# Side-by-side keys for one score product, paired global scores, and earlier q and k loads in a fused attention and expert kernel

## The chip, the cores and the metric

The kernel runs on one core of one Trainium2 chip. The metric is device time in microseconds (us) of one execution; before the change its median over three runs is 869.57 us (868.72 to 870.97). The core has five engines that run in parallel, each through its own list of instructions in order: TensorE (PE, matrix products; PEld is its loading of weights), VectorE (DVE), ScalarE (ACT), GpSimd (POOL), and SyncE (SP), which here only issues DMAs.

## The reference, cut to what matters

```
def _attn_ref(q, k, v, sampled_blocks):          # B, H, S, D = 4, 8, 768, 64; blocks of 32 rows
    scores = scale * np.matmul(q, k.transpose(0, 1, 3, 2))
    mask = np.abs(blk_i - blk_j) <= 1
    mask = mask | (blk_i == 0) | (blk_j == 0) | (blk_i == n_blocks - 1) | (blk_j == n_blocks - 1)
    mask[...] = True                              # and three sampled key blocks for each query block
    attn = softmax(np.where(mask, scores, -1e9))
    return np.matmul(attn, v)

def reference(...):
    x = attn_out.transpose(0, 2, 1, 3).reshape(B * S, H * D)
    return _moe_ref(x, ...)   # top-2 of 8 experts by x @ w_gate and noise, each relu(x @ w1[e]) @ w2[e]
```

A query block sees eight key blocks: its neighbours and itself (three), three sampled ones, and the first and the last. Queries of the first and last block (the global ones) see all 768 keys.

## The kernel before

The attention comes first and takes the first third of the time, then the experts. The work of attention is a list of items in fixed order (`items`, L64): for each batch 12 query items `("q", b, t, f)`, which are a tile `t` of 128 queries (four blocks) and a half `f` of the eight heads, and four global items `("g", b, i, par)`. There are 64 items, 16 to a batch. `steps` walks through them as a software pipeline with one step for each item. A step at item k first turns the probabilities of item k (`turn`, on PE, copied out by DVE and ACT), then computes the scores of item k+2 and their softmax (`scores`, `soft`), then the product with V of item k-1 (`av`) and its scaling (`norm`). Between these parts a router for the experts is woven in by small slices (`background`), and its table of one-hot products (`hot`, L748 on POOL, L757 on PE) shares POOL, DVE and PE with the attention.

The scores of a query item (`scores`, L232) are 16 products of 192 columns on 64 rows and 32 columns of the array (head dimension 64, one block of 32 queries), over two strips of the keys: the three neighbouring blocks and a copy of the three sampled blocks; and then four products of 64 columns on 64 rows and all 128 columns of the array for the first and last key block. Each float32 product stands as two instructions in the trace. A global item (`scores`, first branch) is four products of 384 columns on one half of the array's rows. Each item takes two of six PSUM banks for its scores.

POOL copies the sampled blocks of a tile two tiles ahead into rows behind the keys (`prefetch_k`, L194, three copies for each block) and scales q (L175). `soft` takes the maximum on DVE (L278, L269) and the exponential on ACT (L281, L273). SP issues all loads in program order: q (`prefetch_q`, L186), the keys of the next batch in six parts (`load_k`, L164), V of a tile in two halves (`prefetch_v`, L206 and L210), where a V tile may be loaded once the product that used its buffer three tiles earlier is done, and the stores of x (L589). For each block of queries V takes three loads of one block each, at a place that SP reads out of a register; 264 of SP's loads are of that kind. In the last batch there are two V buffers, and SP also issues the zero fill of the output (L1277) and the first expert weights (L852).

## Time and profile before

| what | us |
|---|---|
| median of three runs | 869.57 |
| the profiled execution's own time | 876.67 |
| its span, first to last instruction | 874.8 |
| PE busy | 812.1 |
| DVE busy | 562.1 |
| ACT busy | 357.9 |
| POOL busy | 346.6 |
| last score product of the attention (L232) starts | 301.3 |

An engine's list runs in order, so a wait on one instruction holds up all behind it. "x" counts instructions, a stretch gives start and length in us from the start of the span, and square brackets give the idle time before a row and what ended it. PEclk is the granted clock of TensorE as a share of 2.4 GHz.

### The profile page before, as it was taken

To read this page: it belongs to the slowest core of one execution; us is meant where nothing else is said; L and a number is where in the kernel's file an instruction comes from. 1 tells how busy PE (TensorE), PEld (TensorE's weight loads), DVE (VectorE), ACT (ScalarE), POOL (GpSimd) and SP (SyncE) were. 2 spreads that over 40 slices of the span, in tenths; PEclk is the share of its full clock that TensorE was granted. 3 is DMA by queue.
4 is the path that set the end of the run, shared out by engine and by line. 5 is a ranking of instruction groups with operands and counts; after the bars stand their busy time and mean duration, and the time that the engine had idled before them with its cause. 6 is when DMAs were issued, how large, how long until landed. Compare 5 with 4: busy or idle time off the path is not lost.

```text
span 874.8 us, 26176 instructions
## 1 busy us (share of the span) xinstructions
PE 812.1 (93%) x10207; PEld 513.8 (59%) x10207; DVE 562.1 (64%) x1197; ACT 357.9 (41%) x666; POOL 346.6 (40%) x584
## 2 busy tenths in 40 slices
PE   7988988989887869999989899999999999999996
PEld 5776776677665657565467454554554554554552
DVE  6576885888786537762123368688688697696631
ACT  4655654755654405321022242452452552642510
POOL 3444455545547330131133606516516426322311
PEclk7899998999999969999999999999999999999998
DMA  4677687667688895755139959729739629523301
GB/s 155 196 210 203 175 222 198 200 184 219 185 263 265 232 196 151 195 185 107 50 100 196 242 123 231 202 80 238 202 98 230 196 90 246 171 67 126 101 28 51
DMA packets 119847, 148.94 MB, mean 170 GB/s; under 512 B 69515, under 2 KB 76300, under 8 KB 119714
## 3 DMA queue, kind: packets, MB, share of 16 engines
q1 hardware_dynamic: 107490, 109.22, 48.1%
q0 software_dynamic: 12224, 37.96, 13.4%
q8 instruction: 82, 1.34, 0.6%
q14 instruction: 51, 0.42, 0.2%
HBM read 107.28 MB, written 26.15 MB: 153 GB/s over the span
## 4 chain that ended last, share of the span: by engine, by line
PE 71%; DVE 8%; issue 7%; SPq 6%; DMA 3%; POOL 2%; ACT 1%; another core or an unknown queue 1%; POOLq 1%; DVEq 0%; ACTq 0%
PE pc L1086 28%; PE pa L1039 9%; PE pa L1000 6%; PE ps L232 6%; PE pd L1039 5%; PE pd L1000 4%; SPq L210 4%; PE po L327 3%; PE pc L1039 2%; PE pc L1095 2%; DMA kk<-in_kt_dram 2%; DVE m L278 2%; PE ps L305 2%; PE po L397 1%
## 5 line engine op out<-in xcount | busy, mean ns | idle before, releaser
L1086 PE MATMUL pc<-w,hh 128*128 128x512 f16 x768 | 228.4, 379 | 0.0
L1119 POOL DMA_INDIRECT out_dram<-y,r_xT x46 | 66.9, 1454 | 216.4 <-DVE y L1118 179.1
L1086 PE MATMUL pc<-w,hl 128*128 128x512 f16 x384 | 145.5, 379 | 0.0
L1086 PEld LDWEIGHTS <-hh 128*128 128x128 f16 x768 | 74.5, 98 | 86.4
L1039 PEld LDWEIGHTS <-w 128*128 128x128 f16 x840 | 82.2, 98 | 63.1
L281 ACT ACTIVATE p<-ps,m 128x256 f32<-128x256 f32 x192 | 75.2, 474 | 80.2 <-DVE m L278 73.8
L278 DVE TENSOR_REDUCE m<-ps 128x2 f32<-128x512 f32 x96 | 61.7, 684 | 33.6 <-PE ps L232 33.5
L232 PE MATMUL ps<-kk,q 64*32 64x192 f32 (+1 forms) x1920 | 77.9, 340 | 4.6 <-POOL q L175 2.8
L194 POOL COPY kk<-kk 128x128 f32 x264 | 67.0, 303 | 37.8 <-DMA kk<-in_kt_dram 21.4
L1008 ACT ACTIVATE hh<-pa 128x408 f16<-128x408 f32 (+2 forms) x60 | 26.1, 447 | 123.8 <-PE pa L1000 104.1
L890 DVE SCALAR_TENSOR_TENSOR w<-wraw,w 128x1024 f16<-128x1024 f32 (+1 forms) x58 | 65.2, 1127 | 15.7 <-ACT w L886 15.7
L232 PEld LDWEIGHTS ps<-kk,q 64*32 64x32 f32 (+1 forms) x1920 | 52.5, 129 | 31.4 <-issue 20.4
L1011 DVE SCALAR_TENSOR_TENSOR hl<-pa,hh 128x408 f16<-128x408 f32 (+2 forms) x60 | 29.9, 503 | 60.1 <-ACT hh L1008 47.7
L327 PE MATMUL po<-va,ptr 128*32 128x68 f32 x1536 | 56.1, 235 | 9.6 <-DVE xr L337 2.8
L1086 PEld LDWEIGHTS <-hl 128*128 128x128 f16 x384 | 37.5, 98 | 45.3
L942 POOL DMA_INDIRECT xg<-x_rows,r_xT x46 | 57.2, 1242 | 14.7 <-issue 14.7
L960 POOL DMA_INDIRECT pv<-out_dram,r_xT x44 | 48.1, 1093 | 32.4 <-issue 29.8
L886 ACT ACTIVATE w<-wraw 128x1024 f16<-128x1024 f32 (+1 forms) x58 | 56.4, 975 | 7.0 <-DMA wraw<-in_moe_w_dram 7.0
L327 PE MATMUL po<-vb,ptr 128*32 128x68 f32 x1536 | 55.4, 232 | 1.9 <-issue 1.8
L1118 DVE SCALAR_TENSOR_TENSOR y<-pc,r_xT,pv 128x512 f32<-128x512 f32 x37 | 27.7, 750 | 45.0 <-PE pc L1086 45.0
L305 PE MATMUL ps<-r_ident,p 128*128 128x128 f32 x384 | 53.9, 283 | 2.3 <-ACT p L281 1.2
L1000 PEld LDWEIGHTS <-w1s 128*128 128x128 f16 x432 | 42.9, 100 | 19.1 <-issue 6.3
(229 smaller groups left out, 1531.2 us busy)
## 6 DMA issues: line engine op xcount, KB each, us to landing
wraw<-in_moe_w_dram SPq DMA_DIRECT2D x64, 512.0 KB
va<-in_vw_dram SPq DMA_DIRECT2D x40, 384.0 KB
vb<-in_vx_dram SPq DMA_DIRECT2D x176, 64.0 KB
q<-in_qt_dram SPq DMA_DIRECT2D x24, 256.0 KB
va<-in_vx_dram SPq DMA_DIRECT2D x88, 64.0 KB
kk<-in_kt_dram SPq DMA_DIRECT2D x18, 256.0 KB
x_rows<-x SPq DMA_DIRECT2D x16, 256.0 KB
out_dram<-zeros SPq DMA_DIRECT2D x4, 768.0 KB
```

What stands on the lines that cost most here:

```text
L194: nc.gpsimd.tensor_copy(kk[:, self.row(t, j) + n], flat[:, bass.ds(self.listed(t * self.NJ + j, n), P)])
L232: mm = lambda o, l, r: nc.tensor.matmul(o, l, r, start=True, stop=True, skip_group_check=True)
L278: nc.vector.tensor_reduce(m[:, par], s[par].rearrange("p (e c) -> p e c", e=2), axis=AX.X, op=ALU.max, negate=True)
L281: nc.scalar.activation(p[:, 2 * e + par], s[par][:, 256 * e:256 * e + 256], AF.Exp, bias=m[:, par, e:e + 1])
L305: nc.tensor.transpose(t[:, e, c], p[:, 2 * e + par, P * c:P * c + P], self.ident)
L327: nc.tensor.matmul(o[32 * j:32 * j + 32, h], d[:, h % 2, h // 2, x, 32 * j:32 * j + 32], self.values(v[:, self.slot(t, j)], 4 * f + h), st ...
L890: self.nc.vector.scalar_tensor_tensor(lo, t, WS, hi, op0=ALU.mult, op1=ALU.subtract)
L942: nc.gpsimd.indirect_dma_start(out=self.xg[0:m, c + self.place(u)], out_offset=None, in_=self.x_dram[0:nr], in_offset=bass.IndirectOffsetO ...
L1000: nc.tensor.matmul(ph[:, 0:m], w[:, wt, slot, kb % 2 * P:kb % 2 * P + P], r["xt"][:, kb, a, o:o + m], start=i == 0, stop=i == last)
L1039: nc.tensor.matmul(o, w[:, wt, slot, s * P:s * P + P], mv(s, a), start=i == 0 and p in tail, stop=i == 5, skip_group_check=True)
L1086: nc.tensor.matmul(py, h[:, f, o], w(f)[:, x], start=i == 0, stop=i == last)
L1119: d = nc.gpsimd.indirect_dma_start(out=self.out, out_offset=bass.IndirectOffsetOnAxis(ap=r["ix"][0:m, c:c + 1], axis=0), in_=y[0:m], in_of ...
```

## The change

Five things change. The keys that a block of queries sees lie side by side in new tiles `kc` (two, for even and odd tiles of queries): POOL copies three sampled blocks as before and one more piece of three neighbouring blocks, and ACT copies the first and last block, once for each batch and each of the two tiles. A query item's scores are then 16 products of 256 columns, and the four products of 64 columns are gone. The two global items of one `i` are scored in one step, with the products of both halves of the array's rows in turn, and the order of items is changed so that the four global items of a batch follow each other (in the first batch, one query item stands between the pairs). q is loaded a step earlier in most tiles and each part of the next batch's keys one step earlier. The rest makes room: `kk` is smaller, some tiles move between pools, and the zeros for the fill are made in an x buffer at step 49 in place of a tile of their own at step 18.

```diff
-            self.items += g[0:2] + q[0:1] + g[2:3] + q[1:2] + g[3:] + q[2:] if b == 0 else q[0:1] + g[0:3] + q[1:2] + g[3:] + q[2:]
+            self.items += g[0:2] + q[0:1] + g[2:] + q[1:] if b == 0 else q[0:1] + g + q[1:]
...
-        self.kk = [two(2 - 2 * i).tile([P, self.NB + 2 * J * 3, P], F32, name=f"kk{i}") for i in range(2)]
+        self.kk = [two(2 - 2 * i).tile([P, self.NB, P], F32, name=f"kk{i}") for i in range(2)]
+        self.kc = [self.buf.tile([P, J, self.NP, 8, 32], F32, name=f"kc{i}") for i in range(2)]
...
     def prefetch_k(self, b, t):
-        nc, kk = self.nc, self.kk[b % 2]
-        js = self.real(t)
+        nc, kk, kc, NB = self.nc, self.kk[b % 2], self.kc[t % 2], self.NB
         flat = kk.rearrange("p n c -> p (n c)")
-        for j in js:
+        turned = lambda x: x.rearrange("p e (n c) -> p n e c", c=32)
+        for j in self.real(t):
+            blk = t * self.NJ + j
             for n in range(3):
-                nc.gpsimd.tensor_copy(kk[:, self.row(t, j) + n], flat[:, bass.ds(self.listed(t * self.NJ + j, n), P)])
-
-    def row(self, t, j):
-        return self.NB + ((t % 2) * self.NJ + j) * 3
+                nc.gpsimd.tensor_copy(kc[:, j, :, 3 + n], flat[:, bass.ds(self.listed(blk, n), P)].rearrange("p (n c) -> p n c", c=32))
+            nc.gpsimd.tensor_copy(kc[:, j, :, 0:3], turned(kk[:, blk - 1:blk + 2]))
+        for j in range(self.NJ if t < 2 else 0):
+            nc.scalar.activation(kc[:, j, :, 6:8], turned(kk[:, 0:NB:NB - 1]), AF.Copy)
...
-            i, h = it[2], head(it[3])
-            qg = self.st["qg", b]
-            s = self.st[it, "s"] = [self.bank() for _ in range(2)]
+            i, qg = it[2], self.st["qg", b]
+            s = [[self.bank() for _ in range(2)] for _ in range(2)]
             for kh in range(2):
                 for e in range(2):
-                    mm(s[kh][64 * e:64 * e + 64, 0:384], qg[h, 2 * i + e, :],
-                       kk[h, NB // 2 * kh:NB // 2 * kh + NB // 2, 2 * i + e])
+                    for par in range(2):
+                        mm(s[par][kh][64 * e:64 * e + 64, 0:384], qg[head(par), 2 * i + e, :],
+                           kk[head(par), NB // 2 * kh:NB // 2 * kh + NB // 2, 2 * i + e])
+            for par in range(2):
+                self.st[it[:3] + (par,), "s"] = s[par]
             return
         _, b, t, f = it
         q = self.st["q", b, t]
         self.st[it, "s"] = [self.bank() for _ in range(2)]
         s = [x.rearrange("p (e c) -> p e c", e=2) for x in self.st[it, "s"]]
+        kc = self.kc[t % 2].rearrange("p j n e c -> p j n (e c)")
         for e in range(2):
             p = 2 * f + e
             for j in range(self.NJ):
-                blk = min(max(t * self.NJ + j - 1, 0), NB - 3)
                 for par in range(2):
-                    w = kk[head(par), blk:blk + 3, p]
-                    step = (self.row(t, self.slot(t, j)) - blk) * P
-                    w = bass.AP(tensor=w.tensor, offset=w.offset, ap=[list(w.ap[0]), [step, 2]] + [list(a) for a in w.ap[1:]])
-                    mm(s[par][32 * j:32 * j + 32, e, 0:192], q[head(par), p, 32 * j:32 * j + 32], w)
-        for e in range(2):
-            p = 2 * f + e
-            for par in range(2):
-                mm(s[par][:, e, 192:256], q[head(par), p, :], kk[head(par), 0:NB:NB - 1, p])
+                    mm(s[par][32 * j:32 * j + 32, e], q[head(par), p, 32 * j:32 * j + 32], kc[head(par), self.slot(t, j), p])
...
-            if new[0] != "none":
+            if new[0] == "q" or new[0] == "g" and new[3] == 1:
                 self.scores(new)
-                self.soft(new)
+                for par in range(2 if new[0] == "g" else 1):
+                    self.soft(new[:3] + (par,) if new[0] == "g" else new)
...
-            if new[0] == "q" and new[3] == 1:
-                for _ in range(1 + (nq == self.late_)):
-                    if nq < len(tg):
-                        self.prefetch_q(*tg[nq])
-                        nq += 1
+            if new[0] == "q" and nq < len(tg) and (nq > self.late_) == (new[3] == 1):
+                self.prefetch_q(*tg[nq])
+                nq += 1
...
-            if new[0] == "q" and new[1] + 1 < B and 0 < 2 * new[2] + new[3] - 1 <= 6:
-                self.load_k(new[1] + 1, 2 * new[2] + new[3] - 2, 6)
+            if new[0] == "q" and new[1] + 1 < B and 0 < 2 * new[2] + new[3] <= 6:
+                self.load_k(new[1] + 1, 2 * new[2] + new[3] - 1, 6)
...
+    at(PER * 3 + 1, lambda: nc.gpsimd.memset(spare(), 0.0))
```

In the first batch PE's list has this order from the first global scores on. The names are score banks (`ps`), keys (`kk`, `kc`), global queries (`qg`), queries (`q`), probabilities (`pg`, `p`); x8 and x4 count products. Before:

```order
L232 MATMUL ps<-kk_105,qg_107 64x384 x8
L293 MATMUL ps<-r_ident,pg 96x128 x8
L232 MATMUL ps<-kk_105,q 32x192 x16
L232 MATMUL ps<-kk_105,q 128x64 x4
L293 MATMUL ps<-r_ident,pg 96x128 x8
L232 MATMUL ps<-kk_105,qg_107 64x384 x4
L305 MATMUL ps<-r_ident,p 128x128 x8
L232 MATMUL ps<-kk_105,q 32x192 x16
L232 MATMUL ps<-kk_105,q 128x64 x4
L293 MATMUL ps<-r_ident,pg 96x128 x8
L232 MATMUL ps<-kk_105,qg_107 64x384 x4
L327 MATMUL po<-va_99,ptr 32x68 x4
```

and in the changed kernel, where L238 stands for L232, L294 for L293, L306 for L305 and L328 for L327:

```order
L238 MATMUL ps<-kk_105,qg_109 64x384 x8
L294 MATMUL ps<-r_ident,pg 96x128 x8
L238 MATMUL ps<-kc_107,q 32x256 x16
L294 MATMUL ps<-r_ident,pg 96x128 x8
L306 MATMUL ps<-r_ident,p 128x128 x8
L238 MATMUL ps<-kk_105,qg_109 64x384 x8
L294 MATMUL ps<-r_ident,pg 96x128 x8
L238 MATMUL ps<-kc_107,q 32x256 x16
L328 MATMUL po<-va_99,ptr 32x68 x4
```

The second pair of global scores is one group of eight, and behind it the turning of its first item follows with nothing between.

On SP's list, behind the last V load of the third tile, the first batch's lists differ so (`kk_106` is the keys of the second batch, `qg` and `ends` its global queries and V ends, `va_99` the V buffer of the fourth tile). Before:

```order
L210 DMA vb_104<-in_vx_dram 32x512
L186 DMA q<-in_qt_dram 128x512
L164 DMA kk_106<-in_kt_dram 128x512
L169 DMA qg_108<-in_qg_dram 128x256
L172 DMA ends_110<-in_vg_dram 64x512
L186 DMA q<-in_qt_dram 128x512
L206 DMA va_99<-in_vw_dram 96x2x512
```

and changed (L191 for L186, L169 for L164, L174 for L169, L177 for L172, L212 for L206):

```order
L216 DMA vb_104<-in_vx_dram 32x512
L191 DMA q<-in_qt_dram 128x512
L169 DMA kk_106<-in_kt_dram 128x512
L191 DMA q<-in_qt_dram 128x512
L169 DMA kk_106<-in_kt_dram 128x512
L174 DMA qg_110<-in_qg_dram 128x256
L177 DMA ends_112<-in_vg_dram 64x512
L169 DMA kk_106<-in_kt_dram 128x512
L191 DMA q<-in_qt_dram 128x512
L212 DMA va_99<-in_vw_dram 96x2x512
```

Two more parts of the keys and one more q stand ahead of the V loads of the fourth tile. The last part of the second batch's keys moves from the 89th to the 82nd DMA of SP's list, that of the third batch from the 187th to the 180th, and the last V load of tile (1, 4) from the 186th to the 187th.

## Rows read from the trace of the kernel before

**Rows 1.** Busy time by stretch: length, each engine's busy us (instructions), PEclk, DMA share, GB/s.

```profile
81.00:155.60 74.60, 66.80 (x1654) 51.04 (x1652) 56.75 (x162) 43.63 (x97) 35.42 (x103) 0.95 0.74 202
155.60:225.80 70.20, 64.29 (x1655) 49.61 (x1653) 55.49 (x162) 44.36 (x97) 37.90 (x104) 1.00 0.70 199
255.00:324.60 69.60, 51.69 (x1195) 40.48 (x1180) 41.35 (x122) 25.00 (x60) 32.07 (x59) 0.85 0.84 224
```

**Rows 2.** SP's waits, 28 to 138.5 us: sum in us, times, longest.

```profile
SPq L186 <- DMA va<-in_vw_dram: 1.5, 1, 1.5
...
SPq L206 <- PE ps L232: 1.2, 2, 0.9
SPq L206 <- PE po L327: 1.1, 1, 1.1
```

**Rows 3.** SP's list: start, length, queue, line, DMA, count.

```profile
77.23 0.97 SPq L210 DMA_DIRECT2D vb<-in_vx_dram  x2
...
137.20 1.74 SPq L210 DMA_DIRECT2D vb<-in_vx_dram  x2
138.99 0.42 SPq L164 DMA_DIRECT2D kk<-in_kt_dram  x1
...
146.51 1.32 SPq L210 DMA_DIRECT2D vb<-in_vx_dram  x2
```

**Rows 4.** PE's list: AV products of three tiles, and waits of POOL's making.

```profile
75.81 1.48 PE L232 MATMUL ps<-kk,q 64*32 64x192 f32 x40 [2.25 <-POOL q L175]
...
82.92 0.33 PE L327 MATMUL po<-va,ptr 128*32 128x68 f32 x8
...
141.46 0.33 PE L327 MATMUL po<-va,ptr 128*32 128x68 f32 x8
...
146.95 0.59 PE L757 MATMUL po<-hot 128*128 128x256 f16 x2 [2.76 <-POOL hot L748]
...
148.53 2.58 PE L232 MATMUL ps<-kk,q 64*32 64x192 f32 x40
...
157.07 0.33 PE L327 MATMUL po<-va,ptr 128*32 128x68 f32 x8
```

**Rows 5.** Weight loads of one query item's scores, and what follows.

```profile
101.05 0.51 PEld L232 LDWEIGHTS ps<-kk,q 64*32 64x32 f32 x32
101.86 0.52 PEld L232 LDWEIGHTS ps<-kk,q 64*128 64x128 f32 x8 [0.30 <-issue]
102.45 0.17 PEld L293 LDWEIGHTS ps<-r_ident,pg 128*96 128x96 f32 x2
```

**Rows 6.** Line 232 alone in one wave each: a global item, the first pair.

```profile
85.53:85.85 0.32, 0.32 (x4) 0.14 (x2) 1.00 0.90 199
...
9.02:9.34 0.32, 0.32 (x8) 0.17 (x4) 1.00 0.04 6
```

**Rows 7.** One global item: scores on PE, maxima on DVE, exponentials on ACT.

```profile
90.55 1.51 PE L232 MATMUL ps<-kk,qg 64*64 64x384 f32 x8
...
91.45 1.20 DVE L269 TENSOR_REDUCE mg<-ps 128x1 f32<-128x384 f32 x2
...
92.95 1.05 ACT L273 ACTIVATE pg<-ps,mg 128x384 f32<-128x384 f32 x2 [1.71 <-DVE mg L270]
```

**Rows 8.** POOL's copies of keys: the wait at 142 us, line 194, line 175.

```profile
142.37 0.54 POOL L194 COPY kk<-kk 128x128 f32 x2 [7.48 <-DMA kk<-in_kt_dram]
...
L194 POOL COPY kk<-kk x264: 284/293/1072, 8.6 to 278.2; 128x128 f32 x132
...
L175 POOL TENSOR_SCALAR q<-q x24: 610/617/635, 10.7 to 282.3; 128x512 f32<-128x512 f32 x24
```

**Rows 9.** ACT's copy of 256 columns, by form.

```profile
L383 ACT ACTIVATE x<-xr 128x256 f16<-128x256 f32 x32 | 13.4, 417 | 0.9 <-issue 0.7
```

**Rows 10.** POOL in the last batch.

```profile
267.28 4.05 POOL L194 COPY kk<-kk 128x128 f32 x12
...
271.93 3.03 POOL L748 TENSOR_TENSOR hot<-hot,r_pay 128x512 f16<-128x512 f16 x3
```

More of the change, by code (lines that the diff above doesn't have):

```diff
@@ L87, in open @@
         self.vb = [two(i).tile([P, J, self.HW], F32, name=f"vb{i}") for i in range(3)]
-        self.kk = [two(2 - 2 * i).tile([P, self.NB + 2 * J * 3, P], F32, name=f"kk{i}") for i in range(2)]
+        self.kk = [two(2 - 2 * i).tile([P, self.NB, P], F32, name=f"kk{i}") for i in range(2)]
+        self.kc = [self.buf.tile([P, J, self.NP, 8, 32], F32, name=f"kc{i}") for i in range(2)]
         self.qgt = [two(2 - 2 * i).tile([P, self.NP, 64], F32, name=f"qg{i}") for i in range(2)]
         self.ends = [two(2).tile([P, self.HD], F32, name=f"ends{i}") for i in range(2)]
-        self.xs = [two(n // 2 * 2).tile([P, self.NP, 2, P], F16, name=f"x{n}") for n in range(4)]
+        self.xs = [self.buf.tile([P, self.NP, 2, P], F16, name=f"x{n}") for n in range(2)]
         self.known = self.const.tile([P, self.NB, 2], F32, name="known")
@@ L97, in open, with open_x @@
         nc.vector.memset(self.known, 1.0 / XS)
+    def open_x(self, ctx):
+        p = ctx.enter_context(self.tc.tile_pool(name="axs", bufs=1))
+        self.xs += [p.tile([P, self.NP, 2, P], F16, name=f"x{n}") for n in (2, 3)]
     def bank(self):
@@ L159, in numbers @@
             skip_runtime_bounds_check_because="packed block numbers")
-        return lambda blk, n: ((v[blk - 1] >> 5 * n) & 31 * unit).with_bounds(min_val=0, max_val=self.NB * unit)
+        return lambda blk, n: ((v[blk - 1] >> 5 * n) & 31 * unit).with_bounds(min_val=0, max_val=(self.NB - (unit > 1)) * unit)
     def load_k(self, b, i, n):
@@ L817, in open_left @@
         self.wst = pool("wst", 3)
-        self.w1s = pool("w1s", 2)
-        self.w2p = pool("w2p", 4)
+        self.w1s = [pool("w1s", 1)]
         self.xp = pool("mxp", 1)
@@ L823, in open_left, with open_more @@
         self.nc.gpsimd.memset(self.xg[:, C // P], 0.0)
+    def open_more(self, ctx):
+        for name, bufs in (("w1t", 1), ("w2p", 4)):
+            p = ctx.enter_context(self.tc.tile_pool(name=name, bufs=bufs))
+            if bufs == 1:
+                self.w1s.append(p)
+        self.w2p = p
     def open_right(self, ctx):
@@ L881, in high_piece @@
         else:
-            small = self.w1s if e == 0 and i < 2 else self.zp if e == 1 else None
+            small = self.w1s[i] if e == 0 and i < 2 else self.zp if e == 1 else None
             self.w1b[e, i] = (small.tile([P, 2, 4, 2 * P], F16, name="w1s") if small else
@@ L1252 @@
     att = Attention(tc, qt, qg, kt, vx, vw, vg, sampled_blocks, H, DM // H)
-    late, early, left, right = ExitStack(), ExitStack(), ExitStack(), ExitStack()
+    late, early, left, right, first = (ExitStack() for _ in range(5))
     att.open(late, early, router.ident)
@@ L1271, with spare @@
     UB = 9
-    zeros = []
+    def spare():
+        return att.xs[2].rearrange("p n a c -> p (n a c)")[:, 0:512].bitcast(F32)
     def fill_out(i):
-        z = zeros[0] if i < 4 else ex.xg[:, C // P, 0:512].bitcast(F32)
+        z = spare() if i < 4 else ex.xg[:, C // P, 0:512].bitcast(F32)
         nc.sync.dma_start(out[i * 384:(i + 1) * 384].rearrange("(p n) (h d) -> p (n h) d", p=P, d=256),
                           z[:, None, :].to_broadcast([P, 3 * DM // 256, 256]))
-    def make_zeros():
-        zeros.append(ip.tile([P, 256], F32, name="zeros"))
-        nc.gpsimd.memset(zeros[0], 0.0)
     plan = {}
@@ L1304 @@
     at(14, router.split_gate)
-    at(18, make_zeros)
+    at(7, first.close)
+    at(7, att.open_x, early)
     def step(n, spot):
@@ L1315, in step @@
             f(*a)
-    ip = early.enter_context(tc.tile_pool(name="init", bufs=1))
+    ip = first.enter_context(tc.tile_pool(name="init", bufs=1))
     att.start(ip)
@@ L1320 @@
     late.close()
+    ex.open_more(left)
     ex.open_right(right)
```

## Prediction

> **What bounds the kernel now.** I read the busy time by stretch first, then the lists of SP and PE in time, then the form of single operations.
>
> By stretch [rows 1] the reader sees PE busy 90 and 92% of the second and third batch's time, DVE 76 and 79%, POOL about half: PE looks like the bound, so that a shorter score product should pay in full. SP has no column there, and its waits must be looked for. From 28 to 138.5 us its sums are 1.5 us on a DMA, 1.2 and 1.1 on PE [rows 2], of 110 us: SP issues nearly without pause. It is a second bound beside PE, and the question at each V tile is which of the two comes last. The key load issued at 138.99 was what POOL waited for until 142.37 [rows 3, 8], 3.4 us later; I take that as an estimate of any load's landing. The last V loads of tile (0, 5) are issued by 77.23 + 0.97 = 78.2, so they land at about 81.5, and the AV product starts at 82.92 [rows 3, 4]. Those of tile (1, 4) are issued by 138.94, landing at about 142, and the product starts at 141.46: at the landing, within the estimate. So for the first 140 us V, and with it SP's list, sets the pace; PE's slack in its scores is not worth its length there. In the last batch DMA is 84% busy, the clock 0.85, and PE 74% [rows 1]: several limits take turns.
>
> **The score product of a query item.** Its 32 instructions on 32 columns begin at 101.05, the 8 on 128 columns at 101.86, the next operation at 102.45 [rows 5]: 0.81 + 0.59 = 1.40 us, of which 0.30 is a pause of the weight loader between the two forms. An instruction of 64 rows and 32 columns fills one of eight places of the array, and 32 of them are four waves. After the change 0.59 goes and the 0.81 grows. If all of it grew with the columns, 0.81 x 256/192 = 1.08, a gain of 0.32. A global item shows what columns alone cost: 384 take 0.32 us in a wave [rows 6], so 64 take 0.053, and in four waves 0.21: 1.02, a gain of 0.38. I take 0.35; 48 items make 16.8 us, if PE set the end everywhere.
>
> **The global pair.** One item alone starts two instructions in each 0.32 us, while in the very first pair, which already stood together, four start in the same 0.32 (the counts 4 and 8 also hold those still running) [rows 6]. A pair then takes what one takes now, 1.51 us from first start to last end, about 1.45 to the next operation [rows 7], and a batch saves 2 x 1.45 = 2.9 us. The price is the softmax. In one item the maxima start at 91.45, and the exponentials end at 92.95 + 1.05 = 94.00, which is 2.0 us behind the scores [rows 7]; that latency now lies under an AV product and the turning of another item. In the new order the second pair's first item is turned directly behind its scores: the wait is 2.0 us at least, 2.9 if DVE still copies. The first pair has AV work before it and waits 0.3 to 1.2, and the first query item behind the pairs waits about 0.8 since only a turning and one shorter score stand before its own. Sum 3.1 to 4.9, taken as 4.0: a loss of 1.1 in a batch. The first batch's first pair stood together already.
>
> **POOL and ACT.** POOL gets 88 copies of 384 columns: 128 columns take 0.293 and 512 take 0.617 [rows 8], so about 0.5 each, 2 us in a full tile and 44 us in all. POOL is half idle up to 225.8 [rows 1] and copies two tiles ahead; that idle time hides them. Without that cover they would cost their 2 us in a tile. They do so at one place: in the last batch the key copies run from 267.28 for 4.05 us, and behind them POOL makes the router's table from 271.93, for which PE waits; 2.1 us more stand before it [rows 10]. ACT gets 32 copies of 256 columns at 0.417 [rows 9], 3.3 us in a batch. Those wait for the last part of the next batch's keys, and exponentials and `ptr` copies queue behind: ACT can stand for some us at the end of each of the first three batches, from nothing to about 8 in the first. I count nothing, since the V tiles (0, 4) and (1, 4) are late there anyway.
>
> The Trainium skill, "SBUF — State Buffer", section "Who interferes with whom", holds that a GpSimd operation and a VectorE operation with two SBUF inputs lock each other out in full. The trace has such a copy: the longest of the 264 took 1.072 us, against a median of 0.293 [rows 8]. By that rule copies of 0.5 us would also stop DVE; the rival below prices it.
>
> **q and keys sooner.** The last part of the third batch's keys was issued at 138.99, and POOL stood still for it 7.48 us, until 142.37 [rows 3, 8]. Behind that copy waited the router's table, so PE waited 2.76 us at 146.95, and the next scores took 2.58 us [rows 4], against 1.40 for a group above: about the double, as at half clock. Seven places earlier in SP's list, at 0.5 to 0.9 us each (0.97 and 1.74 for two [rows 3]), is 3.4 to 6 us: POOL is then free by 136 to 139, and the wait goes. What is late next is V of tile (1, 5), issued by 146.51 + 1.32 and landing at about 151.2, while its product starts at 157.07 [rows 3, 4]: 5.9 us of room. Worth: 2.8 for the wait, 1.1 for the score and as much for the AV group behind it at half clock, less 0.5 for what remains: 4.5 us. The same edit takes the wait of 2.25 us at 75.81 away, for q behind POOL's key copies [rows 4], but there tile (0, 5) is bound by V, and V's places in the list don't move forward: 1.5 us at most are to be had, the 82.92 against 81.5 above. Two key parts and a q more stand before tile (0, 3): three issues of 0.42 [rows 3]; the places behind them in the list are the old ones within one, so 0 to 1.3.
>
> **The sum**, as the advance of PE against before, at the profiled execution's own pace. It took 876.67 us, 1.9 of that outside its span of 874.8; the median of the runs is 7.1 lower, and I take the difference off that median.
> - Up to AV of (1, 0): bounded by SP, 1.5.
> - Up to AV of (1, 4): SP's waits on PE, 1.2 and 1.1, can shrink [rows 2], its list has one DMA more: 0.5 more, so 2.0.
> - End of the second batch: 4.5, so 6.5.
> - Third batch: 12 x 0.35 = 4.2, less 1.1 for the global items, less about 1 where DVE at 79% now ends later than PE: 2.1, so 8.6.
> - Last batch: 12 x 0.35 halved, since the router's work on DVE and the fills set much of it, 2.1; less 1.1; less 2.1 for the copies: -1.1, so 7.5.
>
> The experts' part is not touched. 869.6 - 7.5 is 862 us.
>
> **Rivals.**
> 1. *PE paces everything.* SP's remaining waits and the landing's uncertainty give way, and the 16.8 us count in full: 16.8 + 4.5 + 2.25 - 4.4 - 2.1 - 2 = 15, or 855. For it: PE's 92%. Against: SP's list has hardly a gap.
> 2. *The exposed softmax, slower than before.* The wait of up to 2.9 us between a pair and its turning, with little on PE for 4.9 in all, drops the clock in each batch as the pause before 148.53 did; half clock then costs about 2.2 us, as priced above. Loss in a batch 4.9 + 2.2 - 2.9 = 4.2; all four make 16.8, and POOL's 2.1 comes on top: 18.9 against 1.5 + 4.5 + 8.4 (24 query items of the second half of the attention, the first half being SP's) = 14.4. That is 874. It decides once the loss in a batch is over 3.1. Against it: at 90.55 the latency is 2.0, not 2.9.
> 3. *The last batch gives it back.* DMA at 84% moves the fills, V and weights at its own pace, and what was won before is waited for at the last V tiles: 1 to 2 us remain, 868. Against: the fills move forward with their steps.
> 4. *The lock.* If one of the 88 copies in four meets such an operation (a guess, from DVE being busy three quarters of that time), it stops DVE for 0.5 us and is itself held for 0.8: 22 x 1.3 = 29 us of POOL and DVE, half of it on PE's path in the dense batches: 14, or 876. Against: the median of line 194's copies is only 9 ns above the shortest, 284 [rows 8]. The page of the Trainium skill named above would have it so.
> 5. *The side-by-side product gains nothing,* since its waves are held by weight loads (0.51 us for 32 [rows 5], the same 32 as now): then the 0.32 to 0.38 shrinks to 0, 4.2 + 2.1 less, 868. Against: the loads end before the second half of the waves.
>
> **How the numbers follow.** Chances: the forecast 0.57, rival 1 0.12, rival 2 0.10, rival 3 0.12, rival 4 0.03, rival 5 0.06. The forecast's own range, with each term at its bounds, is 857 to 866. It is widened down to 854, to take in the middle of rival 1, and up to 871, to take in rivals 3 and 5; what is left out is rivals 2 and 4 and half of rival 1, 0.19. About 0.3%, 2.6 us, is what a measurement of this kernel tells from no change. Faster by more: the forecast but a little, rival 1, and a part of 3 and 5, 0.73. Within: the most of 3 and 5, a little of 2, 0.16. Slower: 0.11.
>
> **What would show it.** Score groups of 1.0 to 1.1 us to the next operation on PE, and 32 records in place of 40; a pair of global items in 1.5; a new wait of 2 to 3 us before the turning of the first item of each second pair; no POOL wait of 7 us before the third batch's key copies; SP's waits on PE still short until 140 us; AV of (1, 4) no more than 4 us earlier. Wrong would be: score groups over 1.3 us; POOL's copies of 384 columns at 0.8 us or more; DVE waiting beside them; AV of (3, 0) less than 5 us earlier, or the first expert product not earlier at all.

## The result, and the profile after

The changed kernel takes 876.53 us in the median of 20 runs (870.30 to 881.26), the kernel before 869.43 (20 runs, 862.05 to 880.17). The ratio is 1.0072, with a 95% interval of 1.005 to 1.0094: slower by 0.7%, 6 to 7 us, where 862 was forecast, a gain of 0.9%. 876.53 lies outside the range of 854 to 871.

Busy time by stretch, after, to be held against [rows 1]; columns are the stretch, its length, each engine's busy us (instructions), PEclk, DMA share and GB/s:

```profile
81.00:155.60 74.60, 61.83 (x1624) 45.76 (x1622) 61.25 (x165) 48.80 (x108) 47.74 (x129) 0.98 0.70 197
155.60:225.80 70.20, 58.53 (x1510) 44.01 (x1512) 59.65 (x161) 45.71 (x103) 48.03 (x127) 0.97 0.71 201
255.00:324.60 69.60, 48.51 (x1179) 37.30 (x1178) 40.05 (x116) 24.52 (x59) 33.44 (x66) 0.83 0.80 213
```

PE did lose work: its busy share falls from 90 and 92% to 83 and 83%. But DVE's rises from 76 and 79% to 82 and 85%, POOL's from 47 and 54% to 64 and 68%.

PE's list of after, four places (start, length, engine, line, operation, count, [idle before it and who ended it]):

```profile
100.01 1.09 PE L238 MATMUL ps<-kc,q 64*32 64x256 f32 x32
101.04 1.08 PE L294 MATMUL ps<-r_ident,pg 128*96 128x128 f32 x8
...
239.83 1.52 PE L238 MATMUL ps<-kk,qg 64*64 64x384 f32 x16
...
243.03 0.31 PE L294 MATMUL ps<-r_ident,pg 128*96 128x128 f32 x1 [1.67 <-ACT pg L274]
...
278.30 0.38 PE L757 MATMUL po<-hot 128*128 128x256 f16 x2 [3.19 <-POOL hot L748]
```

A query item's scores take 101.04 - 100.01 = 1.03 us to the next operation, against 1.40 [rows 5], and a pair of global items 1.52 against 1.51 for one item [rows 7]: both products came out as worked out. The new wait behind a pair is there, 1.67 us, a little under the 2.0 to 2.9 forecast. The time did not follow.

Where the time was lost is seen in the last batch. Before, the second AV product of tile (3, 0) starts at 251.70 and stands ahead of the router's products (lines 681 to 685), which wait for DVE:

```profile
250.29 1.47 PE L232 MATMUL ps<-kk,q 64*32 64x192 f32 x40
251.70 0.33 PE L327 MATMUL po<-va,ptr 128*32 128x68 f32 x8
...
254.43 1.51 PE L232 MATMUL ps<-kk,q 64*32 64x192 f32 x40
257.67 0.20 PE L681 MATMUL po<-r_O,r_tri 128*128 128x48 f16 x1 [1.74 <-DVE xr L337]
```

After, it starts at 260.34, behind them:

```profile
250.54 1.09 PE L238 MATMUL ps<-kc,q 64*32 64x256 f32 x32
251.56 1.09 PE L306 MATMUL ps<-r_ident,p 128*128 128x128 f32 x8
252.59 1.09 PE L238 MATMUL ps<-kc,q 64*32 64x256 f32 x32
258.31 0.20 PE L681 MATMUL po<-r_O,r_tri 128*128 128x48 f16 x1 [4.63 <-DVE r_O L668]
258.34 0.29 PE L683 MATMUL po<-r_O,r_ones 128*128 128x40 f16 x5
258.49 0.20 PE L685 MATMUL po<-r_Rh,r_ones 128*128 128x48 f16 x1
260.34 0.46 PE L328 MATMUL po<-va,ptr 128*32 128x68 f32 x8 [1.66 <-DVE r_A L689]
```

Both pairs now stand between the first and the second query item of a batch, so the second query item comes one step later in the list. In the last batch, where the router's steps are dense, one step decides: its AV product falls behind a chain of DVE operations that lets PE go on at 258.31 and again at 260.34. PE stands for 4.63 + 1.66 us, and with these waits the granted clock is 0.50 from 256 to 266 us (the lower of its two levels, 1.2 GHz), against 0.83 in the same ten us before. Behind that AV product, with a global item's product (line 354) that follows it, a V buffer comes free. SP's list before:

```profile
251.83 0.34 SPq L186 DMA_DIRECT2D q<-in_qt_dram  x1
253.52 0.34 SPq L206 DMA_DIRECT2D va<-in_vw_dram  x1
```

and after:

```profile
251.84 0.34 SPq L191 DMA_DIRECT2D q<-in_qt_dram  x1
263.53 0.34 SPq L212 DMA_DIRECT2D va<-in_vw_dram  x1
```

V of tile (3, 2), the next DMA behind the same load of q, is asked for 10 us later. That this costs more on top isn't shown: from 225 to 330 us PE waits 4.5 us for V in the changed kernel, and 1.6 and 6.1 us in the two profiles of the kernel before. The first expert product starts at 329.97 instead of 324.64. From there to the end after is 4 us shorter (546.2 against 550.2 of the span) in these two executions; in the profiles of the experiments that part, whose code is not touched, took 541.5 to 559.0, so I build nothing on it.

### The profile page after: what moved, and what is told of

Its sections match the earlier page's. It is cut to its first block, busy times and chain, and to the rows that moved or that the text cites. A ratio compares the mean times of both kernels' runs of the same rounds, so it can differ in the third digit from the quotient of the medians.

```text
span 876.2 us, 25615 instructions
## 1 busy us (share of the span) xinstructions
PE 787.8 (90%) x9823; PEld 490.2 (56%) x9823; DVE 572.2 (65%) x1197; ACT 367.3 (42%) x698; POOL 388.1 (44%) x672
## 5 line engine op out<-in xcount | busy, mean ns | idle before, releaser
L200 POOL COPY kc<-kk 128x128 f32 x264 | 70.8, 308 | 24.7 <-PE ps L238 18.5
L328 PE MATMUL po<-va,ptr 128*32 128x68 f32 x1536 | 61.2, 240 | 21.1 <-DVE r_xT L399 6.2
L328 PEld LDWEIGHTS po<-va,ptr 128*32 128x32 f32 x1536 | 43.2, 117 | 41.6 <-issue 19.1
L238 PE MATMUL ps<-kc,q 64*32 64x256 f32 x1536 | 59.1, 405 | 7.0 <-POOL q L180 3.6
L328 PE MATMUL po<-vb,ptr 128*32 128x68 f32 x1536 | 60.3, 236 | 4.5 <-issue 4.4
L306 PE MATMUL ps<-r_ident,p 128*128 128x128 f32 x384 | 56.5, 294 | 2.4 <-ACT p L282 2.4
L1006 PE MATMUL pd<-xta,w 128*128 128x408 f16 (+1 forms) x144 | 46.3, 330 | 6.1 <-DVE hl L1017 6.0
```

The lines of the kernel that those rows point to most:

```text
L200: nc.gpsimd.tensor_copy(kc[:, j, :, 3 + n], flat[:, bass.ds(self.listed(blk, n), P)].rearrange("p (n c) -> p n c", c=32))
L238: mm = lambda o, l, r: nc.tensor.matmul(o, l, r, start=True, stop=True, skip_group_check=True)
L306: nc.tensor.transpose(t[:, e, c], p[:, 2 * e + par, P * c:P * c + P], self.ident)
L328: nc.tensor.matmul(o[32 * j:32 * j + 32, h], d[:, h % 2, h // 2, x, 32 * j:32 * j + 32], self.values(v[:, self.slot(t, j)], 4 * f + h), st ...
```

## The experiments

The change has three parts: side-by-side keys (K), pairs of global items in the new order (P), and sooner q and k (S). They were taken apart, with 6 or 12 runs of each kernel. K always brings along the moves that make room, which were not run alone. The jobs ran on chips on which the kernel before itself took 868 to 885 us, so ratios to the runs of before beside each are compared, with 95% intervals:

| parts | ratio |
|---|---|
| S | 0.9950 (0.9914 to 0.9987) |
| P | 1.0084 (1.0049 to 1.0119) |
| K | 1.0091 (1.0057 to 1.0124) |
| K + S | 0.9979 (0.9952 to 1.0005) |
| K + P | 1.0104 (1.006 to 1.0149) |
| K + P + S (the change) | 1.0072 (1.005 to 1.0094) |
| K + S, and P in the first three batches | 0.9974 (0.9941 to 1.0007) |

**K alone.** The changed kernel with the edits of the next two experiments together.

> Of the three parts only the side-by-side keys: score groups of a q item are one product of 256 columns, while the global items stand alone and in the order of before, and q and k are loaded when before loads them. Theory 1 (the pairs' order makes a chain of the last batch late): the whole loss is the pairs', and this kernel is at least level with before: 862 to 869 us, first expert product at 319 to 325. Theory 2 (q and k sooner push V back in SP's full list): the loss is the loads', so this is also 862 to 869, with V of tiles (1,4) and (2,4) landing within 1 us of before. Theory 3 (POOL's 88 copies delay q's scaling and the hot counts): this keeps the loss, 873 to 877, with a hot wait of about 3 us in the last batch. Theory 4 (the score product is not what sets the pace, so its 0.35 us buys nothing): within 0.3% of before, 867 to 872, although each score group takes 1.0 us.

1.0091: slower by itself, which of the four only theory 3 allowed. Its POOL list, the third batch's keys (compare [rows 8]):

```profile
143.62 0.78 POOL L200 COPY kc<-kk 128x128 f32 x3 [6.55 <-DMA kk<-in_kt_dram]
144.35 0.51 POOL L201 COPY kc<-kk 128x384 f32<-128x384 f32 x1
...
148.20 2.04 POOL L747 TENSOR_TENSOR hot<-hot,r_pay 128x512 f16<-128x512 f16 x2
150.21 0.62 POOL L180 TENSOR_SCALAR q<-q 128x512 f32<-128x512 f32 x1
```

POOL waits for the late keys as before, and then has the longer copies to make before the router's table and q. (In the last batch the wait for that table is 1.66 us, not the 3 expected.)

**K + S.** The changed kernel without the pairs (single products, the step's condition of before), in the order of before:

```
-            self.items += g[0:2] + q[0:1] + g[2:] + q[1:] if b == 0 else q[0:1] + g + q[1:]
+            self.items += g[0:2] + q[0:1] + g[2:3] + q[1:2] + g[3:] + q[2:] if b == 0 else q[0:1] + g[0:3] + q[1:2] + g[3:] + q[2:]
```

> The changed kernel with the global items single and in the order of before; side-by-side keys and the sooner q and k stay. Theory 1: the pairs' order cost 5 us at the experts' start, so 869 to 872, the second AV product of tile (3,0) at 250 to 253 and ahead of the router's chain there, first expert product near 325. Theory 2: V still lands 3 to 5 us later than before at (0,3), (1,3) and (2,3), and the time stays at 874 to 878. Theory 3: also 874 to 878.

0.9979, better than theory 1 asked for; its second AV product of (3, 0) starts at 247.9. The pairs cost 0.0093, about 8 us, on top of this.

**K + P.** The changed kernel with the loads of before:

```
-            if new[0] == "q" and nq < len(tg) and (nq > self.late_) == (new[3] == 1):
-                self.prefetch_q(*tg[nq])
-                nq += 1
+            if new[0] == "q" and new[3] == 1:
+                for _ in range(1 + (nq == self.late_)):
+                    if nq < len(tg):
+                        self.prefetch_q(*tg[nq])
+                        nq += 1
...
-            if new[0] == "q" and new[1] + 1 < B and 0 < 2 * new[2] + new[3] <= 6:
-                self.load_k(new[1] + 1, 2 * new[2] + new[3] - 1, 6)
+            if new[0] == "q" and new[1] + 1 < B and 0 < 2 * new[2] + new[3] - 1 <= 6:
+                self.load_k(new[1] + 1, 2 * new[2] + new[3] - 2, 6)
```

> The changed kernel with q and k loaded when before loads them; side-by-side keys and the pairs stay. Theory 1: stays at 874 to 878, the second AV product of (3,0) at 259 to 261. Theory 2: 866 to 870, with V of (0,3), (1,3) and (2,3) landing within 1 us of before's 55.4, 126.2 and 196.3. Theory 3: 874 to 878, and POOL waits again 5 to 7 us for the third batch's keys near 140.

1.0104, with that product at 263.7, later than the 259 to 261 expected. Theory 2, that the sooner loads are the loss, falls: by it this kernel, without them, would have taken 866 to 870 us, 0.996 to 1.001 times before. With K the sooner loads gain 1.0091 - 0.9979, over 1%; with K + P they gain 0.0032, which the intervals can't tell from nothing.

**P out of the last batch alone.** K and S stay, and P in the first three batches; in the last batch the products are single again, in this order:

```
...
+            elif b == self.B - 1:
+                self.items += q[0:1] + g[0:3] + q[1:2] + g[3:] + q[2:]
...
```

> The changed kernel with only the last batch's global items put back: single, and in the order of before (three of them ahead of the second q item, one behind it). Theory 1: 870 to 872, that is 4 to 6 us less than the changed kernel; second AV product of (3,0) back at 249 to 253, the V load of (3,2) triggered at 252 to 254 instead of 262. Theory 2 and theory 3: 875 to 877, since neither SP's list of the first three batches nor POOL's copies are touched.

0.9974: the pairs' loss is in the last batch. PE's list there:

```profile
248.97 0.33 PE L334 MATMUL po<-va,ptr 128*32 128x68 f32 x8
...
252.25 1.09 PE L243 MATMUL ps<-kc,q 64*32 64x256 f32 x32
256.26 0.20 PE L687 MATMUL po<-r_O,r_tri 128*128 128x48 f16 x1 [2.91 <-DVE xr L344]
```

The AV product stands ahead of the router's products again, at 248.97, and V of (3, 2) is asked for at 251.34. In the other three batches the pairs neither gain nor lose anything that can be told (0.9974 against 0.9979).

**The kernel before, once more.**

> The kernel before, unchanged, for a second profile: the first one took 876.67 us, 7 above the median, so the places where it stood against the changed kernel's profile are to be seen again. If the first profile was unlucky in one place, that place shows here: second AV product of tile (3,0) at 245 to 249 instead of 251.7, or first expert product at 319 to 322 instead of 324.6. If the 7 us lie in the experts' part, the attention's times are the same within 1.5 us.

Second AV product of (3, 0) at 249.2, first expert product at 324.2: the first profile was 2.5 us late in the one and level in the other.

**S alone.** The lines of `prefetch_q` and `load_k` in `steps` (the + and - of K + P above, turned round), in the kernel before.

> The kernel before with only the sooner loads of q and k; scores as 32 + 8 products, single global items, order of before. The recorded prediction (sooner keys are worth 4.5 us, since POOL's wait of 7.5 us for the third batch's keys goes): ratio 0.993 to 0.996 to the runs of before beside it. Theory A (the sooner loads are what makes the side-by-side keys bearable, because POOL and ACT then copy the next batch's keys in time; they are worth 10 us only together with those copies): 0.994 to 1.000 here. Theory B (sooner loads are worth about 10 us of themselves, as the step from the kernel with side-by-side keys alone, 1.0091, to that with sooner loads, 0.9979, would read if the parts only added): 0.987 to 0.990.

0.9950, the 4.5 us of the prediction. POOL still waits for the third batch's keys, 6.56 us, but until 139.21 in place of 142.37 [rows 8]. PE's wait for the router's table behind it (2.76 us at 146.95 [rows 4]) is gone, and the next score group takes 1.47 us in place of 2.58; from 148 to 151 us the granted clock is 1.00, where before it was 0.50 from 148.5 to 151.2.

**P alone.** The `items` line, the joint score products and the step's condition, in the kernel before.

> The kernel before with only the global items in pairs and in the changed order; scores, loads as before. Theory 1 (the pairs' order costs some 8 us in the last batch, whatever the other parts are): 1.006 to 1.011 times before, second AV product of (3,0) near 259 and behind the router's chain. Rival (the pairs cost that only where the shorter scores bring the last batch's work closer together): 0.998 to 1.003.

1.0084, with that AV product at 259.88, behind the router's products as in the changed kernel. The rival falls: it needs no shorter scores.

**Pairs around the second query item.** The changed kernel with

```
-            ... if b == 0 else q[0:1] + g + q[1:]
+            ... if b == 0 else q[0:1] + g[0:2] + q[1:2] + g[2:] + q[2:]
```

> The changed kernel with another order of the pairs in batches two to four: first query item, first pair, second query item, second pair. Both pairs stay single products; the second query item comes two steps sooner than in the changed kernel and one sooner than before. Theory 1 (the loss is the place of the second query item in the last batch): 0.994 to 0.999 times before, V of (3,2) triggered at 250 or sooner, and the wait before the turning of the second pair's first item gets shorter than 1.6 us, since the second query item's turning and AV product stand before it. Rival (the loss is the pair itself, four banks at once and two items' exponentials behind each other): 1.005 to 1.010, with the wait in place.

1.0009 (0.9975 to 1.0042): most of the loss goes, as theory 1 has it, but it asked for 0.994 to 0.999, and the wait did not get shorter:

```profile
248.51 1.11 PE L294 MATMUL ps<-r_ident,pg 128*96 128x128 f32 x8 [2.02 <-ACT pg L274]
```

Its second AV product of (3, 0) starts at 254.0, between the two, and stands ahead of the router's products (262.36). The single items in the new order, which would part the order from the pairs altogether, were not run. What holds the rest isn't shown; that execution, 890.6 us, was 7 over the median of this kernel.

**Are POOL's copies what eats K's gain?** K + S with the neighbours' copies in the first batch only:

```
-            nc.gpsimd.tensor_copy(kc[:, j, :, 0:3], turned(kk[:, blk - 1:blk + 2]))
+            if b == 0:
+                nc.gpsimd.tensor_copy(kc[:, j, :, 0:3], turned(kk[:, blk - 1:blk + 2]))
```

> Side-by-side keys, sooner loads, single global items in the order of before (0.9979 times before as measured), but POOL's 128x384 copies of the three neighbouring keys are made in the first batch alone; in the other three batches those columns hold the first batch's keys. It prices the copies. Theory L (POOL's copies cost: VectorE's operations with two SBUF inputs stand until a run of POOL operations ends, as the 3.08 us at 116.58 of the changed kernel shows for an operation that takes 0.17 to 0.25 alone, and POOL's later operations come later): 0.987 to 0.993 times before, 4 to 9 us less than with the copies, and the min of a global item's two maxima back at 0.3 us in the mean. Theory S (the shorter score product is worth nothing here, since V, DVE and the last batch set the pace, so that free copies change nothing): 0.996 to 1.000.

0.9968 (0.9939 to 0.9998), hardly ahead of 0.9979: theory S. With the keys there in time, POOL's 44 us are hidden, as forecast, and K still gains nothing over S alone (0.9950). Where the win went in this execution, in PE's list at tile (2, 4):

```profile
208.26 1.13 PE L239 MATMUL ps<-kc,q 64*32 64x256 f32 x32
209.32 0.31 PE L327 MATMUL po<-va,ptr 128*32 128x68 f32 x4
215.35 0.44 PE L327 MATMUL po<-va,ptr 128*32 128x68 f32 x2 [5.72 <-DMA va<-in_vx_dram]
```

PE comes 6 us sooner than in S alone (215.2) and stands 5.72 us for V.

The same copies left out of K alone:

> Side-by-side keys alone (loads and global items as before; 1.0091 times before as measured), with the neighbours' copies made in the first batch alone, as above. Theory L with POOL's delay (the loss of 8 us is POOL's copies, which stand behind the late last part of the next batch's keys and ahead of the hot counts): 0.994 to 1.001. Rival E (the loss is ACT's copies of the two end blocks, which wait for the same late keys with exponentials behind them): 1.006 to 1.010.

0.9980 (0.9949 to 1.0011) against 1.0091: the loss of K alone is the copies, where the keys come late. It also bounds what the moves that make room can cost.

**The lock between GpSimd and VectorE.** The min of a global item's maxima, in K + S:

```
-            nc.vector.tensor_tensor(m[:, 0:1], m[:, 0:1], m[:, 1:2], op=ALU.min)
+            nc.vector.tensor_scalar(m[:, 0:1], m[:, 0:1], m[:, 1:2], None, op0=ALU.min)
```

> The kernel with side-by-side keys, sooner loads and single global items in the order of before, with one operation written in another form: the min of a global item's two maxima (16 of them) is a tensor_scalar with the second column as its scalar, no longer a tensor_tensor with two SBUF inputs. Theory L: the 5.9 us by which the 16 stood above their shortest go, and half of that stands between scores and exponentials of a global item on the way to PE: 2 to 4 us less, 0.993 to 0.996 times before; the longest of the 16 under 0.4 us. Rival L0 (the scalar's read waits in the same way): the longest stay over 1 us and the time at 0.997 to 0.999. Rival S: they get short and the time stays at 0.997 to 0.999.

All forms of this operation in K + S, ns min/median/max:

```profile
L269 DVE TENSOR_TENSOR mg<-mg x16: 159/212/2652, 11.2 to 243.2; 128x1 f32<-128x1 f32 x16
```

and with the edit:

```profile
L269 DVE TENSOR_SCALAR mg<-mg x16: 212/214/215, 12.1 to 241.5; 128x1 f32<-128x1 f32 x16
```

The stalls go to the last one, although 11 of the 16 run beside a GpSimd operation, and L0 falls; the time, 0.9969 (0.9938 to 0.9999), is 0.001 better, which the interval can't tell from nothing.

**Copies on ACT**, in K + S:

```
-            nc.gpsimd.tensor_copy(kc[:, j, :, 0:3], turned(kk[:, blk - 1:blk + 2]))
+            nc.scalar.activation(kc[:, j, :, 0:3], turned(kk[:, blk - 1:blk + 2]), AF.Copy)
```

> The same kernel (side-by-side keys, sooner loads, single global items in the order of before) with the neighbours' copies on ACT in place of POOL: 88 of 128x384. Theory L: POOL's runs get shorter by 2 us a tile, and ACT takes about 0.58 for each, as for its exponentials of that size, 2.3 us a tile: 0.990 to 0.996 times before. Rival A (ACT's queue delays exponentials and the turned tiles' copies by those 2.3 us a tile, and PE waits): 1.000 to 1.008.

0.9985 (0.9957 to 1.0013): between the two expectations, no difference from POOL that can be told.

**q and k from ACT's queue.** In K + S, and in S beside it, from the first step on:

```
-        self.nc.sync.dma_start(self.kk[b % 2][:, p], self.kt[b][:, p])
+        self.ld.dma_start(self.kk[b % 2][:, p], self.kt[b][:, p])
...
-        self.nc.sync.dma_start(q, self.qt[b, t])
+        self.ld.dma_start(q, self.qt[b, t])
...
     def steps(self, router, done, background):
         nc, T, B = self.nc, self.T, self.B
+        self.ld = nc.scalar
```

> Side-by-side keys, sooner loads, single global items in the order of before (0.9979 times before as measured); the loads of q and k behind the first ones are issued by ACT's queue in place of SP's, 12 of some 100 a batch. Theory V (SP's full list sets when V lands, and takes what the shorter scores win): V of (0,4), (1,4) and (2,4) lands 3 to 5 us sooner, no AV product there waits for V, 0.988 to 0.994 times before. Rival D (DVE and the last batch take it): V lands sooner and the time stays at 0.996 to 1.000. Rival A (ACT, in which a load that waits holds up exponentials, loses it again): 1.000 to 1.006.

> The kernel before with sooner loads (0.995 as measured), the loads of q and k issued by ACT's queue as in the run beside it; scores in 32 + 8 products. Theory V: with SP free the score product is what differs, so this stays 3 to 6 us behind the run with side-by-side keys: 0.993 to 0.998 times before, while that one is at 0.988 to 0.994. Rival D: the two are equal within 0.2%.

0.9971 (0.9941 to 1.0001) with K, 0.9934 (0.9899 to 0.9968) without: K gains nothing again, and if anything loses. V was not 3 to 5 us sooner throughout: the last load of tile (2, 4) is issued 0.7 us sooner than in K + S and 3.4 sooner than in S, that of tile (0, 4) 0.7 sooner and 2.6 later. V's own 14 DMAs a tile, 11.6 us from 198.30 on with K, are most of SP's list there. But from 205 to 216 us, around tile (2, 4), PE's waits hold none for V in either, and its AV product starts at 211.6 with K and 211.3 without. That speaks for rival D.

> Side-by-side keys, sooner loads from ACT's queue, single global items in the order of before, and the min of a global item's two maxima as a tensor_scalar. Theory V with the lock's part (0.9979 to 0.9969 as measured on two chips): 0.986 to 0.993 times before. Rival D: 0.995 to 0.999.

K + S with ACT's queue and the tensor_scalar: 0.9962 (0.9924 to 1.0). Rival D.

**V cut down.** S alone, and K + S, both with the two loads into `vb` left out in the second and third batch:

```
             for n, d in enumerate((va[96:128, j], vb[0:32, j], vb[32:64, j])):
+                if n > 0 and 6 <= b * self.T + t < 18:
+                    continue
```

> The kernel before with sooner loads (0.995 as measured), with the loads of the second and third listed V block (the two into vb) left out in the second and third batch: those rows hold the first batch's values. SP's list then is a third as long there, and V can't be what comes last. It is the base for the run beside it. Theory V: 0.988 to 0.994, AV of (2,4) at 208 to 213. Rival D: 0.993 to 0.996.

> Side-by-side keys, sooner loads, single global items in the order of before, with the same loads of V left out in the second and third batch. Theory V (V's landing took what the shorter scores win in those batches): 24 score groups are 0.38 us shorter, 9 us, less the copies' cost; this is 3 to 7 us ahead of the run beside it at AV of (2,5) and at the first expert product, and 0.3 to 0.8% faster. Rival D (DVE, whose 81 to 83% of these batches is the other full engine, takes it): the two stand within 2 us at AV of (2,5), and within 0.2% in time.

0.9957 (0.9924 to 0.9991) without K, 0.9898 (0.9859 to 0.9938) with it: here alone K gains, 0.6%, just clear of the two intervals and inside theory V's range. S alone gains nothing by it (0.9950 with all of V): by these times V's loads hold up the kernel with K in those batches, and not S. Whether it is their place in SP's list or the fewer bytes (DMA share 0.61 against 0.72 in K + S) this doesn't part. The profiles speak less clearly. From AV of (1, 0) to AV of (2, 5), S with V cut:

```profile
95.10:224.30 129.20, 119.44 (x3118) 92.60 (x3117) 103.92 (x302) 80.78 (x180) 71.74 (x205) 1.00 0.58 164
```

K + S with V cut:

```profile
89.00:217.60 128.60, 112.46 (x2922) 82.03 (x2920) 107.92 (x302) 85.31 (x196) 91.71 (x246) 0.97 0.61 173
```

PE's work is 7.0 us less and the stretch only 0.6 shorter; the lead of 6.7 us at (2, 5) was 6.1 at (1, 0). That execution took 868.57 us, the longest of its kernel's six runs and 7 over their median, so the runs and the profile can't be put together here.

**S from ACT's queue with the tensor_scalar.**

> The kernel before with the sooner loads, those of q and k behind the first ones issued by ACT's queue (0.9934 as measured), and the min of a global item's two maxima as a tensor_scalar in place of a tensor_tensor with two SBUF inputs. If the lock's part is on the way to PE here as well, 0.990 to 0.993; if not, 0.993 to 0.996. It is the candidate that beats both kernels.

0.9936 (0.9902 to 0.997). The operation adds nothing here. S with ACT's queue, 0.9934, and this one are the fastest kernels that compute everything: 0.6% under before, 1.4% under the change. The intervals don't tell them from S alone, 0.9950.

## Why the prediction was wrong

*Sooner q and k, 4.5 us: right in time and at its place.* S alone gives 1 - 0.9950 = 0.5%, 4.4 us, and the wait and the half clock that were to go went. Where the time is won is less clear. In the profile of S alone, the first product of (2, 0) starts 2.7 and 1.1 us sooner than in the two profiles of before (163.9; 166.6, 165.0), but the first expert product at 324.98, no sooner than there (324.64, 324.18). So the 4.4 us rest on the runs' times; the profiles don't show them at the end of the attention.

*The global pair, "a loss of 1.1 in a batch": the step that failed most.* It priced the wait behind a pair (1.67 measured, 2.0 to 2.9 forecast) and the saved product (as forecast), and in three batches no loss can be told. It did not ask what else is in the new order: that the second query item stands one step later, and what PE meets between there and its AV product. In the term of the last batch, "less 1.1", that place cost 0.0093 of 869, 8 us. The working followed the global items, and not the query item that they push back. Rival 2 named the pair and put the loss in the softmax of every batch; rival 3 named the last batch, for its DMA. Rival 4's 876 is the measured time, by luck: once the pairs are out and the keys in time, POOL's copies cost no time that can be told (0.9968 without them, 0.9979 with them).

*The shorter scores: right on PE, wrong as a gain.* 0.37 us in each group, forecast 0.35. Of 16.8 the sum counted 4.2 + 2.1 = 6.3; less 1 for DVE and 2.1 for the copies, 3.2 were left to K. K on top of S is worth about -3 us (0.9979 against 0.9950; 0.9971 against 0.9934), which the intervals can't tell from 0. From AV of (1, 0) to AV of (2, 5), before:

```profile
92.00:227.20 135.20, 121.97 (x3114) 94.30 (x3112) 104.34 (x302) 80.87 (x180) 72.24 (x203) 0.97 0.71 199
```

after:

```profile
92.90:225.10 132.20, 111.86 (x2922) 83.27 (x2922) 112.52 (x301) 86.03 (x198) 91.78 (x246) 0.97 0.71 199
```

PE's busy time falls by 10.1 us, its idle time rises from 135.20 - 121.97 = 13.2 to 20.3, and 3.0 are left. (From S alone to K + S the same stretch goes from 135.4 to 131.5 us; at the first expert product K + S is 1.3 ahead, 323.72 against 324.98.) The forecast's own mark was AV of (3, 0), where PE was to be 8.6 us ahead: its first product starts at 237.4 against 237.9 and 235.4 in the two profiles of before, so in this execution no gain was left before the last batch's pairs began. PE's longest waits, 81 to 226 us, before (sum, times, longest):

```profile
PE po L757 <- POOL hot L748: 3.2, 2, 2.8
PE po L681 <- DVE xr L337: 2.2, 2, 1.1
PE po L397 <- DVE xe L376: 1.5, 2, 0.8
```

after:

```profile
PE po L398 <- DVE xr L338: 6.4, 6, 1.9
PE po L328 <- DVE r_xT L399: 5.3, 4, 2.3
PE ps L294 <- ACT pg L274: 3.5, 3, 1.6
```

The wait for POOL is gone, as the sum had it. In its place PE waits for DVE to read out `po`, the one PSUM buffer that AV, the turned rows and the router share: what PE does in a loop with DVE gets shorter on PE's side alone. In the full lists PE's waits for DVE sum to 7.7 us before and 16.4 after, and to 7.9 in S alone and 11.3 in K + S. The prediction had put "about 1" for DVE in the third batch. DVE is even longer busy, 112.52 against 104.34 us, with no work added: of the 8.2, 5.8 are two stalls shown at the end. V is a second taker (the 5.72 us above, and the 0.6% with V cut down); how the two divide what is lost stays open, and a second `po` buffer was not tried. In the last batch K's 2.1 did not come either: from the second AV product of (3, 0) to the experts it is 75.0 us in the second profile of before and 75.8 both in S and in K + S.

*POOL's copies "hidden": right only with S.* 0.51 us each (forecast 0.5):

```profile
L201 POOL COPY kc<-kk 128x384 f32<-128x384 f32 x65 | 33.3, 512 | 0.0
```

With late keys they cost 1.0091 - 0.9980, 1.1%. In the last batch PE's waits for the router's table sum to 5.0 us (3.19 of them at 278.30), against 2.5 and 0.6 in the two profiles of before: 2.5 to 4.4 more, where 2.1 were forecast.

*The sum.* 7.5 us of gain were forecast, and the loss measured is 7.1. By ratios, with a gain as minus: S -4.4, K on it +2.5 (not told from 0), P on both +8.1, together +6.2. The sum had -4.5 for S and -2.0 up to AV of (1, 4), where it took SP's list as the limit, -3.2 for K and +2.2 for P. P and K are each off by some 6 us; P's loss is clear of the noise; that K stays short of its 3.2 is so just barely, and that K loses time is not.

## What to carry to other kernels

A work item that moves up pushes another one down: before an order is changed, follow the item that is pushed back to the end, its product, the buffer that this frees and the load that waits for the buffer, through the stage where the lists are densest. And an engine at 90% pays for a shorter operation only if its partner in the loop has room: with DVE at 76 to 79% and V's loads close behind, 10 us less work on PE made two batches 3 us shorter.

## What the runs showed of the hardware

A VectorE operation with two SBUF inputs can stand through a whole run of GpSimd operations. In the changed kernel, DVE's list at 116 us:

```profile
116.58 3.08 DVE L655 TENSOR_TENSOR r_dl<-r_mx 128x6 f32<-128x6 f32 x1
```

and POOL's:

```profile
116.27 0.51 POOL L201 COPY kc<-kk 128x384 f32<-128x384 f32 x1
116.72 0.77 POOL L200 COPY kc<-kk 128x128 f32 x3
117.43 0.51 POOL L201 COPY kc<-kk 128x384 f32<-128x384 f32 x1
117.88 0.30 POOL L224 COPY va<-known 128x128 f32<-128x128 f32 x1
118.12 0.30 POOL L224 COPY vb<-known 128x128 f32<-128x128 f32 x1
118.38 0.68 POOL L391 TENSOR_TENSOR x<-xr,x 128x256 f16<-128x256 f32 x1
119.02 0.62 POOL L180 TENSOR_SCALAR q<-q 128x512 f32<-128x512 f32 x1
```

An operation on six columns, 0.15 to 0.28 us in the profiles of all other kernels, takes 3.08 (and 3.08 again at 189.54) and ends at 119.66, with the last of nine GpSimd operations that follow one another without a gap. The Trainium skill, "SBUF — State Buffer", section "Who interferes with whom", has the lock: whoever issues first keeps the shared ports for its whole instruction, and the other blocks. The trace agrees, and adds that the loser did not get its turn between two of the winner's operations. This is rival 4's mechanism, seen. It isn't new with K: in the kernel before, the min of a global item's maxima, 0.16 us at its median, takes up to 1.71.

What it cost in time is not settled. With the stalls of the min taken out, 0.001 was won, within the interval; those of other operations were not taken out. Two of them are on the chain for which PE waits 4.63 us in the changed kernel's last batch, beside GpSimd's fill of zeros (256.38 to 257.34) and its scaling of q (257.29 to 257.91):

```profile
256.40 0.95 DVE L658 CAST r_ef<-r_mi 128x12 f32<-128x12 uint32 x1
257.39 0.62 DVE L661 TENSOR_TENSOR r_A<-r_io,r_ef 128x96 f32<-128x96 f32 x1
```

They take 0.17 and 0.26 us there in the kernel before: 1.1 of the 4.63. K + S has the first of them too, 0.98 at 252.87, so it isn't the pairs' loss. As a tensor_scalar with one of the two columns as its scalar, the min took 212 to 215 ns in all 16 cases.
